# Bucketed attention and a rational feed-forward on one core: the order of each pair's work rewritten, one addition per pair on VectorE, a third buffer for high parts

## The chip, the core and the metric

The kernel runs on one core of a Trainium2 chip. The metric is the device time of one execution in microseconds (us). Three runs of the kernel before gave 961.02, 961.62 and 962.98, a median of 961.62. About 0.2% (2 us) is what a measurement of this kernel can tell from no change.

## What is computed

Attention with a mask from hashed buckets, and a feed-forward with a rational function between its two products (the feed-forward's input is the attention's output, 3072 tokens of 512 features):

```
q, k, v: 4 x 8 heads x 768 tokens x 64;  proj: 64 x 6
q_bucket, k_bucket = the 6 signs of q @ proj, of k @ proj, read as a number
scores = q @ k.T / 8, and -1e9 where the buckets differ
attn = exp(scores - rowmax);  attn = attn / (sum + 1e-9);  x = attn @ v
h = x @ w_in  (512 x 2048)
P = a0 + a1 h + a2 h^2 + a3 h^3;   Q = 1 + |b0||h| + |b1| h^2
out = (P / (Q + 1e-6)) @ w_out  (2048 x 512)
```

## The kernel before

**Pairs.** Two heads make a pair; there are 16 pairs (p = 0 to 15), and a pair's 12 steps s are 2 halves of the queries (hf) by 6 tiles of the keys. Every float32 operand of a large product is split into a high part (a cast to float32r, on ScalarE) and a low part (the rest, a subtraction). A pair's work on TensorE, with the names that the profile shows:

- `pss` (`scores`): the 12 score tiles, transposed, 8 matmuls each: high by high, high by low, low by high, and a product of 13 mask rows (`mask_q`, `mask_k`) that adds the bucket penalty and subtracts the row maximum. ScalarE takes the exponential of both heads' halves into `E` (two ACTIVATE). GpSimd adds the exponentials of three steps in a row into `acc`: for each group of three, one addition `acc<-E,E` and one `acc<-acc,E`, each for two heads.
- `psm` (`maxstep`): for the pair after, 12 products of the high parts and mask rows, 4 matmuls each, whose row maxima VectorE takes (TENSOR_REDUCE into `m`). `combine` joins the two halves of `m`, `pst` (`shift_turn`) transposes `m` on TensorE, VectorE writes it as `mt`, and a DMA (`shift_rows`) carries it into row 12 of `mask_q`, for which the last two of the first score tile's 8 matmuls wait.
- `psv` (`values`): the product with v, one PSUM bank for each half hf. `values_out` copies a bank out on ScalarE (`col`, then `xo`), and SyncE's queue stores `xo`.
- `psu` (`sums`): the column sums of the four `acc`; ScalarE copies them out as `sr`.
- `psb` (`bits`): the signs for the next two pairs, at every second pair.

Beside this run the splits of w_in and w_out (`weights`: `wr`, `ws`, `wi_hi`, `wi_lo`, a chain over ScalarE and VectorE) and, in pairs 13 to 15, the loads of the feed-forward's first tokens (`tokens.load`: `xl`, `xh`, `y`). The feed-forward (`Ffn.step`) follows: 96 steps of 12 matmuls `psh` and 12 matmuls `pso`.

**PSUM.** The pool `ps_b` has four banks with one tag: `pss` takes two for each step, and `psv`, `psu`, `pst` and `psh` one each, so a bank must be copied out before a later product gets it. The pool `ps_a` has two double banks, for `psm` and `psb`.

**What sets the order.** Every engine executes its instructions in program order; `keep_in_program_order` (line 94) keeps them so, and so nearly all rows of the profile show that line. The order is a plan: `at(p, s, f, ...)` puts a call at the time 12 p + s, where s may be any number, and all calls are issued in the order of these times. The numbers stand in three tables: `FIRST` (pair 0 and what comes before it), `MID` (all other pairs) and `LAST` (pair 15, the first feed-forward steps). In `MID`, `values=[11.232, 11.235]` puts both halves of `psv` at a pair's end, `values_out=[13.624, 11.651]` copies half 1 out at once and half 0 after the second score step of the pair after, and `maxima` with `maxima_steps` places the 12 `psm` among the `pss`. A number under 12 by little means the end of the pair, where `psv` runs.

**Buffers.** `operand` gives the high parts, low parts and v two buffers each, by the parity of the pair. `LAST["share"] = 11` gives VectorE the second head's additions from the last step of pair 14 on.

Of the kernel before, what the change touches and what calls it, by code (L numbers as in the profile page):

```python
# [8 lines left out]
F32R = mybir.dt.float32r  # L9
# [4 lines left out]
ALU = mybir.AluOpType  # L14
# [4 lines left out]
P = 128  # L19
S = 768  # L20
HQ = 384
NT = S // P
# [3 lines left out]
NPAIR = B * NHP  # L26
# [12 lines left out]
PINNED = ("tensor", "vector", "scalar", "gpsimd", "sync")  # L39
PARTS = 2  # L40
ACCS = 5

MID = dict(
    values=[11.232, 11.235], values_out=[13.624, 11.651], values_store=[16.343, 19.938], maxima=14.842,
    maxima_steps=[-2.469, 0.405, 5.72, -1.821, 2.012, 3.592, 6.656, 5.98, -0.169, 2.19, 3.044, 4.48], sums=11.885,
    sums_store=23.222, high=[11.3, 11.31], low=[11.4, 11.41], bits=11.165, penalties=11.256, maskrows=11.73, load_v=11.882,
    shift_turn=11.021, shift_rows=11.645, load=13.548, recips=[27.25, 35.733, 50.884],
    weights=[[11.238, 16.003, 11.648, 11.215, 11.243, 12.014, 8.577, 10.628, 84.011], [11.734, 11.024, 8.997, 11.67, 169.938, 19.538, 12.0, 11.386, 11.645]],
    weights_last=[-71.997, -119.997, -119.944, -125.487], combine=11.0,
)  # L50

FIRST = dict(
    maxima1=5.731, rate1=0.618, maxima2=13.527, rate2=0.8, high=[11.6, 11.7], low=[11.8, 11.9], bits=5.355, penalties=11.558,
    maskrows=13.003, load_v=10.702, group=2, values=[4.117, 2.119, 0.719, 4.463, 2.555, 0.675], values_out=1.607,
    high1=[-24.581, -9.069], low1=[-9.075, -7.508], load2=-15.454, load3=-29.223, load4=16.55, penalties1=3.81, maskrows1=5.52,
    weights=[[18.321, 11.519, 4.92, 53.379, 11.911, 106.055, -39.7, 11.558, 22.997], [10.848, 11.998, 30.437, 11.678, 10.699, -4.525, 6.547, 18.997, 11.431]],
    warm=6, warms=[3, 3, 3, 1, 1, 1], maxima00=[-23.897, -20.363, -18.634, -18.631, -17.575, -17.572], shift0=[-15.7, 5.117],
    ahead=3, scores=[-3.723, 19.958, 20.538], pen01=[-14.501, -23.848], comp01=-24.325, load_v0=-15.703, bits1=-14.498,
    comp1=[-9.072, -7.867], maxima0=[-3.224, 4.166, 4.336, -8.151, 3.428, -0.292], turn1=[10.225, 14.098], rows1=[11.995, 15.252],
    combine0=[-17.0, 5.0], combine1=[10.0, 14.0], clear=6.0,  # L60
)

LAST = dict(
    group=6, values=[0.5, 0.106], values_out=0.7, vout14=15.994,
    tokens=[[-0.105, -0.89, -2.003, -10.837], [0.189, 1.726, 6.933, 5.285], [5.282, 0.008, 4.776, -0.407]], terms=-0.578,
    ffn=[10.067, 81.505, 121.388], sums=11.67, wide=12, share=11, third=0, sums14=17.262, sumst14=24.048,
)
TINY = 2.0 ** -80

# [106 lines left out]
def attention(ctx, tc, nc, raw, ps_b, tail, tokens, early, operands_to_terms, ffn, load, QF, KF, v, w_in, w_out, wo_d, ident, cst, ones, prj,  # L176
# [5 lines left out]
    def operand(tag, p, shape, dtype, bufs=2):  # L182
        return opn[(NPAIR - 1 - p) % bufs == 0].tile(shape, dtype, tag=f"{tag}_{p % bufs}", name=f"{tag}_{p}")
# [29 lines left out]
    QH, KH, QL, KL, V, MB, ACC, EXP, AV, MS = ({} for _ in range(10))  # L213
# [10 lines left out]

    def high(p, t):
        F, T, n = ((QF, QH, "qh"), (KF, KH, "kh"))[t]
        T[p] = operand(n, p, [P, S], F32R)
        nc.scalar.copy(T[p], F[p])

    def low(p, t, engine=nc.vector):  # L230
        F, H, T, n = ((QF, QH, QL, "ql"), (KF, KH, KL, "kl"))[t]
        T[p] = operand(n, p, [P, S], F32R)
        engine.tensor_tensor(out=T[p], in0=F[p], in1=H[p].bitcast(F32), op=ALU.subtract)

    def bits(p, which=(0, 1)):
# [26 lines left out]
    def halves(banks, p, units, left, right):  # L262
        for u, (a, b) in enumerate(units):
            for h in range(2):
                r = slice(64 * h, 64 * h + 64)
                nc.tensor.matmul(banks[h][:, 0:HQ], a[p][r, left], b[p][r, right], start=(u == 0), stop=(u == len(units) - 1))
# [84 lines left out]
    def scores(p, s):  # L351
        hf, kt = divmod(s, NT)
        e = EXP[p, s] = E[(12 * p + s) % NE if p < NPAIR - 1 else s % LONE]
        late = 12 * (p - NPAIR + 2) + s
        if late >= LAST["wide"] and late % 3 != LAST["third"]:
            both = ps_a.tile([P, 2, 512], F32, tag="psa", name=f"pss{p}_{s}")
            banks = both[:, 0, :], both[:, 1, :]
        else:
            banks = [ps_b.tile([P, 512], F32, tag="s", bufs=4, name=f"pss{p}_{s}_{h}") for h in range(2)]
        halves(banks, p, ((KH, QH), (KH, QL), (KL, QH), (MK, MQ)), slice(kt * P, kt * P + P), slice(hf * HQ, hf * HQ + HQ))  # L360
        for h in range(2):
            nc.scalar.activation(e[:, h, 0:HQ], banks[h][:, 0:HQ], AF.Exp, scale=1.0 / 8.0)
        n = NT // PARTS
        if kt % n == 1:
            ACC[p, hf, kt // n] = sm.tile([P, 2, HQ], F32, tag="acc", name=f"acc{p}_{hf}_{kt // n}", bufs=ACCS)
        if kt % n > 0:
            acc = ACC[p, hf, kt // n]
            x = EXP[p, s - 1] if kt % n == 1 else acc
            for h in range(2):
                engine = nc.vector if h and late >= LAST["share"] else nc.gpsimd  # L370
                engine.tensor_tensor(out=acc[:, h, :], in0=x[:, h, 0:HQ], in1=e[:, h, 0:HQ], op=ALU.add)

    def values(p, s):
        hf, kt = divmod(s, NT)
        if kt == 0:
            AV[p, hf] = ps_b.tile([P, 512], F32, tag="s", bufs=4, name=f"psv{p}_{hf}")
        e = EXP[p, s]
        for h in range(2):
            nc.tensor.matmul(AV[p, hf][64 * h : 64 * h + 64, 0 : HQ + 1], V[p][:, kt, 64 * h : 64 * h + 64],
                             e[:, h, 0 : HQ + 1], start=(kt == 0), stop=(kt == NT - 1))  # L380
# [89 lines left out]
    def at(p, s, f, *args):  # L470
        plan.setdefault(12 * p + s, []).append((f, args))

    def spread(p, steps, gen):
        for s in steps:
            at(p, s, lambda g: next(g, None), gen)

    for p in range(NPAIR):
        mid = 0 < p < NPAIR - 1
        n = (FIRST if p == 0 else LAST)["group"]
        for s in range(12):  # L480
            if p > 0 or s >= FIRST["ahead"]:
                at(p, s, scores, p, s)

            if p > 1:
                at(p - 2, MID["maxima"] + MID["maxima_steps"][s] if p > 2 else FIRST["maxima2"] + FIRST["rate2"] * s, maxstep, p, s)
            if mid:
                at(p, MID["values"][s // NT], values, p, s)
            elif s % n == n - 1:
                for i in range(s - n + 1, s + 1):
                    at(p, s + (FIRST if p == 0 else LAST)["values"][s // n], values, p, i)  # L490
            if s % NT == NT - 1:
                at(p, LAST["vout14"] if (p, s) == (NPAIR - 2, 11) else MID["values_out"][s // NT] if mid
                   else s + (FIRST if p == 0 else LAST)["values_out"], values_out, p, s // NT)
        for hf in range(2):
            at(p, MID["values_store"][hf] if mid else 6 * hf + 9, values_store, p, hf)
        if p < NPAIR - 1:
            at(p, MID["sums"] if p < NPAIR - 2 else LAST["sums14"], sums, p)
            at(p, MID["sums_store"] if p < NPAIR - 2 else LAST["sumst14"], sums_store, p)
        if p > 1:
            for t in range(2):  # L500
                at(p - 2, (MID if p > 2 else FIRST)["high"][t], high, p, t)
                at(p - 2, (MID if p > 2 else FIRST)["low"][t], low, p, t, nc.vector if p > 2 else nc.gpsimd)
            if p % 2 == 0:
                at(p - 2, (MID if p > 2 else FIRST)["bits"], bits, p)
                at(p - 2, (MID if p > 2 else FIRST)["penalties"], penalties, p)
            at(p - 2, (MID if p > 2 else FIRST)["maskrows"], maskrows, p)
        if p > 0:
            at(p - 1, (MID if p > 1 else FIRST)["load_v"], load_v, p)
        if p > 1:
            at(p - 1, MID["combine"], combine, p)  # L510
            at(p - 1, MID["shift_turn"], shift_turn, p)
            at(p - 1, MID["shift_rows"], shift_rows, p)
        if p > 3:
            at(p - 4, MID["load"] if p > 4 else FIRST["load4"], load, p)
        if p % NHP == NHP - 1 and p + 1 < NPAIR:
            spread(p, MID["recips"], recips(p // NHP))
# [303 lines left out]
```

## Time and profile before

| | before |
|---|---|
| median of 3 runs | 961.62 us |
| the profiled execution, its own time | 961.61 us |
| its span (first to last instruction) | 959.8 us |
| TensorE busy | 935.1 us (97%) |
| VectorE busy | 832.1 us (87%) |
| ScalarE busy | 653.3 us (68%) |
| GpSimd busy | 398.3 us (41%) |
| mean granted TensorE clock | 0.994 |

Some 1.8 us of the execution's time lie outside the span. TensorE is busy nearly all of the time, but its ends are modelled: a matmul that waits for a bank right behind another one shows as a longer matmul, not as idle time. So the start times of matmuls are read below, not the busy share.

### The profile page before, as it was taken

The page shows a single profiled execution, that of the slowest core. Times are in us where ns is not written, and L with a number is a line of the kernel's source. Part 1 is how long each engine was busy: PE and PEld are TensorE (multiplying, and loading weights), DVE is VectorE, ACT ScalarE, POOL GpSimd, SP SyncE. Part 2 cuts the span into 40 slices and gives each one's busy share as a digit, 9 for nine tenths or more (in the row PEclk, how much of TensorE's full clock was granted, in tenths as well). Part 3 has the DMA queues.
Part 4 walks back from the last instruction along what each step waited for, and adds up shares of the span by engine and source line. Part 5 has one row for each costly group of instructions (what it writes and reads, how often), then busy time and mean ns, then how long its engine had stood idle before and what let it go on. Part 6 is the DMA issues. An engine that isn't in the chain of part 4 may idle for free.

```text
span 959.8 us, 15893 instructions
## 1 busy us (share of the span) xinstructions
PE 935.1 (97%) x5846; PEld 721.9 (75%) x5846; DVE 832.1 (87%) x1051; ACT 653.3 (68%) x1225; POOL 398.3 (41%) x373
## 2 busy tenths in 40 slices
PE   8989999999999999799999999999999999999997
PEld 4566776767676767568888788888888888888886
DVE  6787878878787878569999899899989999998995
ACT  4566676767776767378766767777677667767664
POOL 6686565656565656332222232222322222232222
PEclk9999999999999999899999999999999999999999
DMA  6134444444444424145700400120030004001001
GB/s 191 41 113 140 139 140 141 140 141 140 140 140 128 143 90 136 55 142 207 238 27 0 133 1 1 59 74 0 1 109 25 1 1 131 1 1 45 1 1 44
DMA packets 39245, 81.51 MB, mean 85 GB/s; under 512 B 7168, under 2 KB 18036, under 8 KB 39168
## 3 DMA queue, kind: packets, MB, share of 16 engines
q1 hardware_dynamic: 38736, 80.27, 26.3%
q8 instruction: 46, 0.75, 0.3%
q14 instruction: 31, 0.25, 0.1%
q10 hardware_dynamic: 432, 0.23, 0.1%
HBM read 56.82 MB, written 21.17 MB: 81 GB/s over the span
## 4 chain that ended last, share of the span: by engine, by line
PE 92%; ACT 2%; DMA 2%; DVE 1%; issue 1%; SPq 1%; POOL 0%; ACTq 0%; POOLq 0%
PE psh L94 27%; PE pso L94 27%; PE pss L94 14%; PE psv L94 13%; PE psm L94 6%; PE psu L94 2%; ACT E L94 2%; PE psb L94 1%; DVE m L94 1%; DMA out<-o 1%; SPq L94 1%; DMA qkf<-kT 1%; DMA wo_d<-wr 1%; PE pst_None L94 0%; POOL acc L94 0%
## 5 line engine op out<-in xcount | busy, mean ns | idle before, releaser
L94 POOL TENSOR_TENSOR gl<-c,gh 128x512 fp32r<-128x512 f32 x96 | 136.3, 1420 | 385.4 <-ACT gh L94 375.8
L94 PE MATMUL pso<-wo,gh 128*128 128x512 f32 x768 | 235.5, 389 | 1.3 <-ACT o L94 1.3
L94 ACT ACTIVATE E<-pss 128x384 f32<-128x384 f32 x384 | 167.4, 491 | 81.9 <-PE pss L94 75.7
L94 DVE TENSOR_REDUCE m<-psm 128x2 f32<-128x768 f32 x192 | 177.9, 956 | 24.3 <-PE psm L94 17.4
L94 POOL TENSOR_TENSOR acc<-E,E 128x384 f32<-128x384 f32 x124 | 126.7, 1044 | 160.3 <-ACT E L94 158.9
L94 PEld LDWEIGHTS pso<-wo,gh 128*128 128x128 f32 x768 | 144.1, 188 | 31.5 <-ACT o L94 1.7
L94 PE MATMUL psh<-xh,wi_hi 128*128 128x512 f32 x384 | 149.6, 390 | 0.0
L94 PE MATMUL psh<-xl,wi_hi 128*128 128x512 f32 x384 | 149.4, 389 | 0.0
L94 PE MATMUL psh<-xh,wi_lo 128*128 128x512 f32 x384 | 149.4, 389 | 0.0
L94 PE MATMUL pso<-wo,gl 128*128 128x512 f32 x384 | 148.4, 389 | 0.0
L94 ACT ACTIVATE h<-psh 128x512 f32<-128x512 f32 x96 | 57.4, 598 | 128.5 <-PE psh L94 128.5
L94 DVE SCALAR_TENSOR_TENSOR c<-c,ab,r 128x512 f32<-128x512 f32 x96 | 136.7, 1424 | 0.0
L94 PE MATMUL psv<-E,v 128*64 128x385 f32 x768 | 131.4, 495 | 0.0
L94 POOL TENSOR_TENSOR acc<-acc,E 128x384 f32<-128x384 f32 x123 | 122.4, 1018 | 5.7 <-ACT E L94 5.5
L94 PEld LDWEIGHTS psv<-E,v 128*64 128x64 f32 x768 | 71.3, 139 | 52.8 <-issue 34.0
L94 PE MATMUL pss<-qh,kh 64*128 64x384 f32 x384 | 90.8, 358 | 2.4
L94 DVE SCALAR_TENSOR_TENSOR w<-h,absb,w 128x512 f32<-128x512 f32 x96 | 75.0, 782 | 17.9 <-ACT w L94 17.6
L94 PE MATMUL pss<-mask_q,mask_k 64*128 64x384 f32 x384 | 81.0, 337 | 3.2 <-DMA mask_q<-mt_None 3.2
L94 PE MATMUL pss<-ql,kh 64*128 64x384 f32 x384 | 83.9, 345 | 0.0
L94 PEld LDWEIGHTS psh<-xh,wi_hi 128*128 128x128 f32 x384 | 72.1, 188 | 15.7 <-issue 0.9
L94 PEld LDWEIGHTS psh<-xh,wi_lo 128*128 128x128 f32 x384 | 72.1, 188 | 15.2
L94 PEld LDWEIGHTS pso<-wo,gl 128*128 128x128 f32 x384 | 72.0, 188 | 15.1
(89 smaller groups left out, 1674.0 us busy)
## 6 DMA issues: line engine op xcount, KB each, us to landing
wr<-w_in SPq DMA_DIRECT2D x16, 512.0 KB
wr<-w_out SPq DMA_DIRECT2D x16, 512.0 KB
wo_d<-wr SPq DMA_DIRECT2D x16, 512.0 KB
wo<-wo_d SPq DMA_DIRECT2D x16, 512.0 KB
qkf<-qT SPq DMA_DIRECT2D x16, 384.0 KB
qkf<-kT SPq DMA_DIRECT2D x32, 192.0 KB
v<-v SPq DMA_DIRECT2D x16, 384.0 KB
x_d<-xo SPq DMA_DIRECT2D x32, 192.0 KB
```

What stands on the lines that cost most here:

```text
L94: return self.tc.keep_in_program_order(issue(*args, **kwargs))
```

## The change

- The tables `MID`, `FIRST` and `LAST` have new numbers throughout: the same calls at other places. In `MID`, half 1 of `psv` now comes before half 0 (`values`), `pst` stands between them (`shift_turn`), both halves are copied out before the next pair's scores (`values_out`), one `psm` stands behind each `pss` (`maxima_steps`), and the cast of k's high part comes after the tenth score step (`high`). In `LAST`, the first three feed-forward steps stand behind all score and value products of pair 15 (`ffn`).
- The addition of a pair's last exponentials (s = 11, both heads in one instruction of 128 x 768) goes from GpSimd to VectorE for pairs 1 to 14, as a call of its own (`add`).
- The high parts of q and k have three buffers; the low parts of even pairs lie in the pool `raw`, under the tags that the tokens' `y` also uses.

```diff
+VADDS = (11,)
 MID = dict(
-    values=[11.232, 11.235], values_out=[13.624, 11.651], values_store=[16.343, 19.938], maxima=14.842,
-    maxima_steps=[-2.469, 0.405, 5.72, -1.821, 2.012, 3.592, 6.656, 5.98, -0.169, 2.19, 3.044, 4.48], sums=11.885,
+    values=[11.684, 11.138], values_out=[11.884, 11.615], values_store=[14.41, 17.811], maxima=14.89,
+    maxima_steps=[1.089, 3.351, 2.636, 5.192, -0.277, 4.26, 7.788, 8.138, -2.212, 6.928, -0.974, 1.717], sums=11.894,
...
 LAST = dict(
...
-    ffn=[10.067, 81.505, 121.388], sums=11.67, wide=12, share=11, third=0, sums14=17.262, sumst14=24.048,
+    ffn=[167.535, 769.59, 808.64], sums=855.873, wide=12, share=11, third=0, sums14=17.126, sumst14=808.331,
...
     def high(p, t):
         F, T, n = ((QF, QH, "qh"), (KF, KH, "kh"))[t]
-        T[p] = operand(n, p, [P, S], F32R)
+        T[p] = operand(n, p, [P, S], F32R, 3)
...
     def low(p, t, engine=nc.vector):
         F, H, T, n = ((QF, QH, QL, "ql"), (KF, KH, KL, "kl"))[t]
-        T[p] = operand(n, p, [P, S], F32R)
+        own = (NPAIR - 1 - p) % 2 == 0
+        T[p] = operand(n, p, [P, S], F32R) if own else raw.tile([P, S], F32R, tag=f"lo{t}", name=f"{n}_{p}", bufs=1)
...
-        if kt % n > 0:
+        if kt % n > 0 and not (s in VADDS and 0 < p < NPAIR - 1):
...
+    def add(p, s):
+        acc = ACC[p, s // NT, s % NT // (NT // PARTS)]
+        nc.vector.tensor_tensor(out=acc, in0=acc, in1=EXP[p, s][:, :, 0:HQ], op=ALU.add)
...
+            if mid and s in VADDS:
+                at(p, MID["adds"][VADDS.index(s)], add, p, s)
```

What the numbers do to the order stands in the following rows, in which a name ends with a running number. TensorE first, at the end of pair 7 (`psv7_0`, `psv7_1` are its halves, each row two matmuls; `pst8` and `psm8` belong to pair 8). Before:

```order
L94 MATMUL psm8_6_2973<-mask_k2_166,mask_q2_163 128x384 x2
...
L94 MATMUL pss7_11_0_2995<-mask_q1_162,mask_k1_165 128x384
...
L94 MATMUL pst8_None_3010<-cst_76,m0_191 64x128
L94 MATMUL psv7_0_3019<-E0_149,v_7_2739 64x385 x2
...
L94 MATMUL psv7_1_3032<-E6_155,v_7_2739 64x385 x2
...
L94 MATMUL psu7_3073<-acc7_0_0_2784,ones_82 32x384 x2
```

With the change:

```order
L95 MATMUL pss7_11_0_2987<-mask_q1_162,mask_k1_165 128x384
...
L95 MATMUL psm8_7_2999<-mask_k2_166,mask_q2_163 128x384 x2
L95 MATMUL psv7_1_3005<-E6_155,v_7_2692 64x385 x2
...
L95 MATMUL pst8_None_3025<-cst_76,m0_191 64x128
L95 MATMUL psv7_0_3041<-E0_149,v_7_2692 64x385 x2
...
L95 MATMUL psu7_3067<-acc7_0_0_2785,ones_82 32x384 x2
```

The turn `pst8` has moved from before all of `psv` to between its halves, and half 1 runs first.

ScalarE, from the end of pair 7 to the first exponentials of pair 8. Before:

```order
L94 COPY col7_1_3061<-psv7_1_3032 128x1
L94 ACTIVATE xo7_1_3062<-psv7_1_3032,col7_1_3061 128x384
L94 CAST wr15_2958<-ws15_2959 128x512
L94 COPY sr7_3082<-psu7_3073 128x384
L94 ACTIVATE E0_149<-pss8_0_0_3084 128x384
...
L94 ACTIVATE E1_150<-pss8_1_1_3105 128x384
L94 COPY col7_0_3129<-psv7_0_3019 128x1
L94 ACTIVATE xo7_0_3130<-psv7_0_3019,col7_0_3129 128x384
```

With the change:

```order
L95 ACTIVATE xo7_1_3034<-psv7_1_3005,col7_1_3033 128x384
L95 CAST qh_9_3039<-qkf9_2476 128x768
L95 CAST wr15_2764<-ws15_2765 128x512
L95 CAST wi_hi_128<-ws14_2978 128x512
L95 COPY col7_0_3063<-psv7_0_3041 128x1
L95 ACTIVATE xo7_0_3064<-psv7_0_3041,col7_0_3063 128x384
L95 COPY sr7_3076<-psu7_3067 128x384
L95 ACTIVATE E0_149<-pss8_0_0_3083 128x384
```

The copy of half 0 (`xo7_0`) has moved from behind the second score step of pair 8 to before its first.

VectorE between pairs 14 and 15 (`mt15` is the turned maximum of pair 15, `acc14_1_1` the last sum of pair 14, `y0_0` a product of the first tokens). Before:

```order
L94 TENSOR_REDUCE m1_192<-psm15_6_5343 128x2
L94 TENSOR_TENSOR y0_0_5349<-xl0_5161,xh0_5160 128x768
L94 TENSOR_TENSOR acc14_1_1_5363<-acc14_1_1_5363,E11_160 128x384
L94 TENSOR_TENSOR m1_192<-m1_192 128x12
L94 TENSOR_SCALAR mt15_None_5384<-pst15_5382 12x128
```

With the change, and under it the rows of SyncE's queue that lead to the DMA of `mt15`:

```order
L95 TENSOR_REDUCE m1_192<-psm15_7_5366 128x2
L95 TENSOR_TENSOR m1_192<-m1_192 128x12
...
L95 TENSOR_SCALAR mt15_None_5396<-pst15_5394 12x128
...
L95 TENSOR_TENSOR acc14_1_1_5335<-acc14_1_1_5335,E11_160 128x768
...
L95 DMA xl0_3_5426<-x_d3_91 128x512
L95 DMA xh0_3_5425<-r_d0_108 64x512 x2
L95 DMA mask_q0_161<-mt15_None_5396 1x6x128 x2
```

`combine` has moved ahead of the addition of pair 14; on the queue the loads `xl0_3` and `xh0_3` still stand directly ahead of the mask row, as they did before. By the waits in the program, `xl0_3` is issued once the last `psv14` matmul and `acc14_1_1` are done, in both kernels.

## Rows read from the trace of the kernel before

**Rows 1.** The page, part 1: span, and busy time of each engine.

```profile
span 959.8 us, 15893 instructions
...
PE 935.1 (97%) x5846; PEld 721.9 (75%) x5846; DVE 832.1 (87%) x1051; ACT 653.3 (68%) x1225; POOL 398.3 (41%) x373
```

**Rows 2.** Windows by stage: pair 0; 1; 2 to 13; 14 and 15; feed-forward.

```profile
0.00:48.90 48.90, 44.68 (x338) 25.22 (x340) 34.94 (x53) 24.52 (x46) 30.60 (x44) 1.00 0.41 115
48.90:77.80 28.90, 24.93 (x222) 17.48 (x222) 24.66 (x30) 17.56 (x39) 20.26 (x19) 1.00 0.40 125
77.80:375.50 297.70, 295.58 (x2622) 212.82 (x2618) 242.27 (x309) 209.47 (x450) 187.20 (x192) 1.00 0.42 133
375.50:432.60 57.10, 49.73 (x385) 36.39 (x383) 36.56 (x47) 32.37 (x73) 23.96 (x23) 0.91 0.36 111
432.60:957.00 524.40, 520.13 (x2296) 429.97 (x2292) 493.68 (x615) 369.39 (x617) 136.27 (x96) 1.00 0.15 50
```

The columns of Rows 2 are the window and its length, then busy time and instructions of PE, PEld, DVE, ACT and POOL, the granted clock, the DMA share and GB/s.

**Rows 3.** Timeline of TensorE, pair 6's values to pair 8's turn: start, length.

```profile
266.93 7.92 PE L94 MATMUL psv<-E,v 128*64 128x385 f32 x47
...
276.21 0.44 PE L94 MATMUL pss<-qh,kh 64*128 64x384 f32 x2
...
277.37 0.89 PE L94 MATMUL pss<-qh,kh 64*128 64x384 f32 x2
...
285.19 0.34 PE L94 MATMUL pss<-qh,kh 64*128 64x384 f32 x2
...
286.24 0.33 PE L94 MATMUL pss<-qh,kh 64*128 64x384 f32 x2
...
287.45 0.44 PE L94 MATMUL psm<-kh,qh 64*128 64x384 f32 x2
...
290.69 0.43 PE L94 MATMUL pst_None<-cst,m 128*64 128x128 f32 x2
```

**Rows 4.** Timeline of ScalarE in the same stretch.

```profile
277.27 0.88 ACT L94 ACTIVATE E<-pss 128x384 f32<-128x384 f32 x2 [0.39 <-PE pss L94]
...
279.61 0.59 ACT L94 ACTIVATE xo<-psv,col 128x384 f32<-128x384 f32 x1
```

**Rows 5.** Timeline of VectorE: pairs 1, 7, 14 and 15.

```profile
49.64 1.71 DVE L94 CUSTOM_DVE_ANT_0 ws<-wr,ws 128x1024 uint16<-128x1024 uint16 x1 [0.54 <-ACT sr L94]
...
280.56 9.61 DVE L94 TENSOR_REDUCE m<-psm 128x2 f32<-128x768 f32 x10 [0.44 <-PE psm L94]
...
392.37 1.34 DVE L94 TENSOR_TENSOR acc<-acc,E 128x384 f32<-128x384 f32 x1 [1.85 <-POOL acc L94]
...
418.29 0.56 DVE L94 TENSOR_TENSOR acc<-acc,E 128x384 f32<-128x384 f32 x1
```

**Rows 6.** Timeline of TensorE in pair 1.

```profile
54.81 0.40 PE L94 MATMUL pst<-cst,m 128*64 128x128 f32 x2 [1.20 <-DVE m L94]
...
68.25 0.40 PE L94 MATMUL pst_None<-cst,m 128*64 128x128 f32 x2 [2.10 <-DVE m L94]
```

**Rows 7.** Timeline of TensorE between pairs 14 and 15.

```profile
393.94 0.45 PE L94 MATMUL pst<-cst,m 128*64 128x128 f32 x1 [3.99 <-DVE m L94]
...
408.24 1.16 PE L94 MATMUL pss<-mask_q,mask_k 64*128 64x384 f32 x2 [3.17 <-DMA mask_q<-mt_None]
```

**Rows 8.** Windows: the two stretches of low clock (columns as in Rows 2).

```profile
391.00:399.00 8.00, 5.06 (x19) 3.87 (x21) 5.44 (x10) 3.52 (x7) 2.30 (x3) 0.57 0.00 0
408.00:412.30 4.30, 4.03 (x25) 3.77 (x27) 1.98 (x3) 2.54 (x7) 1.01 (x1) 0.60 0.69 204
```

**Rows 9.** Timeline of SyncE's queue: pair 7, and between pairs 14 and 15.

```profile
267.44 1.58 SPq L94 DMA_DIRECT2D mask_q<-mt_None  x2
...
404.46 0.33 SPq L94 DMA_DIRECT2D xl<-x_d  x1
...
406.06 1.55 SPq L94 DMA_DIRECT2D mask_q<-mt_None  x2
```

**Rows 10.** The chain that ended last, between pairs 14 and 15.

```profile
406.06 2.13 DMA mask_q<-mt_None
```

More of the change, by code (lines that the diff above doesn't have):

```diff
@@ L41 @@
 ACCS = 5
+VADDS = (11,)
 MID = dict(
-    values=[11.232, 11.235], values_out=[13.624, 11.651], values_store=[16.343, 19.938], maxima=14.842,
-    maxima_steps=[-2.469, 0.405, 5.72, -1.821, 2.012, 3.592, 6.656, 5.98, -0.169, 2.19, 3.044, 4.48], sums=11.885,
-    sums_store=23.222, high=[11.3, 11.31], low=[11.4, 11.41], bits=11.165, penalties=11.256, maskrows=11.73, load_v=11.882,
-    shift_turn=11.021, shift_rows=11.645, load=13.548, recips=[27.25, 35.733, 50.884],
-    weights=[[11.238, 16.003, 11.648, 11.215, 11.243, 12.014, 8.577, 10.628, 84.011], [11.734, 11.024, 8.997, 11.67, 169.938, 19.538, 12.0, 11.386, 11.645]],
@@ L49 @@
-    weights_last=[-71.997, -119.997, -119.944, -125.487], combine=11.0,
+    values=[11.684, 11.138], values_out=[11.884, 11.615], values_store=[14.41, 17.811], maxima=14.89,
+    maxima_steps=[1.089, 3.351, 2.636, 5.192, -0.277, 4.26, 7.788, 8.138, -2.212, 6.928, -0.974, 1.717], sums=11.894,
+    sums_store=14.997, high=[11.678, 9.702], low=[11.952, 11.874], bits=11.08, penalties=11.084, maskrows=11.881, load_v=11.364,
+    shift_turn=11.469, shift_rows=11.977, load=14.997, recips=[23.927, 35.322, 55.327],
@@ L50 @@
+    weights=[[10.997, 11.997, 11.565, 179.694, 11.509, 11.858, 11.485, 10.284, 865.593], [11.325, 11.725, 11.628, 13.913, 879.87, 11.172, 0.394, 11.155, 11.855]],
+    weights_last=[-134.698, -0.003, -120.0, -869.006], combine=11.172, adds=[11.662],
 )
 FIRST = dict(
-    maxima1=5.731, rate1=0.618, maxima2=13.527, rate2=0.8, high=[11.6, 11.7], low=[11.8, 11.9], bits=5.355, penalties=11.558,
-    maskrows=13.003, load_v=10.702, group=2, values=[4.117, 2.119, 0.719, 4.463, 2.555, 0.675], values_out=1.607,
@@ L55 @@
[L55 to L58, printed above, removed]
@@ L59 @@
-    comp1=[-9.072, -7.867], maxima0=[-3.224, 4.166, 4.336, -8.151, 3.428, -0.292], turn1=[10.225, 14.098], rows1=[11.995, 15.252],
-    combine0=[-17.0, 5.0], combine1=[10.0, 14.0], clear=6.0,
+    maxima1=5.127, rate1=0.677, maxima2=12.804, rate2=0.937, high=[2.549, 0.266], low=[11.68, 11.715], bits=5.525,
+    penalties=9.664, maskrows=10.933, load_v=9.874, group=2, values=[3.491, 1.642, 0.579, 3.401, 2.558, 0.727], values_out=0.891,
+    high1=[-33.057, -32.695], low1=[-31.72, 25.07], load2=-30.033, load3=3.003, load4=33.003, penalties1=3.84, maskrows1=4.581,
@@ new lines @@
+    weights=[[22.225, 9.881, 11.718, 11.891, 11.043, 149.997, 23.169, -56.357, 38.994], [10.211, 12.801, 117.815, -56.338, -54.382, 11.567, -52.133, 11.73, 3.0]],
+    warm=6, warms=[3, 3, 3, 1, 1, 1], maxima00=[-33.07, -33.057, -39.179, -33.066, -39.176, -33.059], shift0=[22.444, 5.568],
+    ahead=3, scores=[25.073, 27.088, 28.003], pen01=[-34.282, -39.151], comp01=-43.535, load_v0=24.263, bits1=-29.13,
+    comp1=[20.074, 22.587], maxima0=[1.293, -0.795, 3.656, 4.864, 3.787, 4.203], turn1=[10.441, 14.104], rows1=[11.9, 16.555],
@@ L61 @@
+    combine0=[-32.349, 4.981], combine1=[10.214, 12.997], clear=-0.607,
 )
 LAST = dict(
-    group=6, values=[0.5, 0.106], values_out=0.7, vout14=15.994,
-    tokens=[[-0.105, -0.89, -2.003, -10.837], [0.189, 1.726, 6.933, 5.285], [5.282, 0.008, 4.776, -0.407]], terms=-0.578,
-    ffn=[10.067, 81.505, 121.388], sums=11.67, wide=12, share=11, third=0, sums14=17.262, sumst14=24.048,
+    group=6, values=[0.134, 0.54], values_out=0.731, vout14=15.036,
+    tokens=[[-0.313, -0.709, -3.003, 0.003], [5.131, 5.728, -1.165, 3.114], [9.008, 3.305, 10.003, -0.13]], terms=-0.174,
```

## The prediction

> **What bounds the kernel now.** The page's first part comes first: TensorE is busy for 935.1 of 959.8 us, VectorE for 832.1, ScalarE for 653.3 and GpSimd for 398.3 [rows 1]. By these shares there would be 25 us to win at most. But a busy share is a mean over stages, and a matmul that waits for a PSUM bank counts as busy, so the next view is the windows by stage [rows 2]. Pairs 2 to 13 take 297.7 us, 24.8 each, with TensorE at 295.58. Pair 0 leaves it idle for 48.90 - 44.68 = 4.2 us, pair 1 for 28.90 - 24.93 = 4.0, pairs 14 and 15 for 57.10 - 49.73 = 7.4 at a granted clock of 0.91, the feed-forward for 4.3 of 524.4. So the feed-forward is at TensorE's own rate, and what an order can give lies in the attention.
>
> Third comes the timeline of TensorE in one pair, for the starts of the matmuls [rows 3]. A score step with its maximum step takes 1.05 us when nothing holds it (285.19 to 286.24). Twelve of them would take 12 x 1.05 = 12.6, yet from the first `pss` at 276.21 to the next pair's `pst` at 290.69 there are 14.48. The stall of 1.9 us hides inside matmuls that read as longer: `pss` at 277.37 shows 0.89 where a free one shows 0.34. ScalarE tells why [rows 4]: half 0 of the values is copied out (`xo`) only at 279.61, behind the exponentials of two steps. Until then one of the four banks is taken, so the scores have three where two steps want four, and each step waits for the exponentials of the one before. A second, smaller part is two `psm` in a row (287.45, 0.44 instead of 0.34), which wait for a bank that VectorE's reduction, 0.96 each [rows 5], has to free.
>
> Fourth, the waits at the edges: in pair 1, `pst` waits 1.20 and 2.10 us for VectorE's `m` [rows 6]; between pairs 14 and 15, 3.99 for `m`, then 3.17 for the DMA of the mask row [rows 7]. After both the clock is low, 0.57 and 0.60 over 8.0 and 4.3 us [rows 8].
>
> **The change, part by part.** The profiled execution took 961.61 us, the median 961.62, so the sum needs no correction; 1.8 us lie outside the span.
>
> *Pairs 2 to 13.* Both copies of the values now stand before the pair's first exponentials, and `sr` too, so the scores start with four banks; one `psm` follows each `pss`, so no doubled step is left. What ends the stall is 14.48 - 12.6 = 1.9 a pair [rows 3]. What can take its place is ScalarE's queue in front of the first exponential. Half 0 now ends with psv: 7.92 us after its start [rows 3]. Then `col`, `xo` (0.59, [rows 4]) and `sr` stand before E, some 1.6 us, and psu covers 1.36 of it (276.21 - 266.93 - 7.92) and the first step 1.05. That fits. VectorE pays more: its last low part (kl, ql) and the new addition stand ahead of the first reduction. By the order it ends them about when the first `psm` is there, so I leave 0.3 of the stall and take 1.6. Twelve pairs: 12 x 1.6 = **19.2**. Ends: 12 x 0.5 = 6, if only the doubled `psm` (2 x 0.27) goes, and 12 x 1.75 = 21.
>
> *The addition.* One instruction of 128 x 768 replaces two of GpSimd. No row shows it; an addition of 128 x 384 took 0.56 alone and 1.34 while GpSimd was at work [rows 5]. Twice that gives 1.1 and 2.7. I take 1.1: GpSimd has two additions less a pair and has ended those of step 10 while psv runs. It costs TensorE nothing as long as it ends before the last group of psu reads it, nine us after the start of psv. Without that cover it would put up to 2.7 us on VectorE's 242.27 / 12 = 20.2 a pair [rows 2] (first rival). Below nothing it cannot go.
>
> *The turn.* `pst` now stands between the halves of psv. So the mask row has half of psv (7.92 / 2), psu (1.36) and the six matmuls that come first in a score tile (0.5, half of a step's twelve in 1.05) as cover: 5.8 us, where all of psv gave it 9.8. SyncE issues one mask row in 0.79 [rows 9], and issue to landing took 2.13 [rows 10]. In the new queue the four rows of `maskrows` stand directly ahead of the turn's two, at every second pair behind v's load too. They wait for the signs, not for the turn, and can go out while half 1 runs. Were all four still to go when `mt` is there, 4 x 0.79 + 2.13 = 5.3 would just fit; with them gone some 2 to 3 us are left. Cost nothing; the cover is the second half of psv, and without it the price is rival B's.
>
> *The third buffer.* It lets k's cast come at the tenth step instead of in psv. It is the same 0.87-sized work on ScalarE, which has 297.7 - 209.47 = 88 us free over the twelve pairs [rows 2]. Nothing by itself; what it takes from psv's stretch is part of the 1.6.
>
> *Pair 1.* VectorE's two long pieces of weights (`ws`, 1.71, [rows 5]) no longer stand ahead of the joined maxima. The waits of 1.20 and 2.10 [rows 6] go, 3.3, and part of the same stall inside the scores, 1.2: **4.5**. Ends 2 (a smaller wait is left) and 5.5.
>
> *Pair 0.* All places are new. Its idle 4.2 us [rows 2] can't all go, since the first loads are in it. Ends: -4 and +2 (a wait of pair 1's size at a new place); I take a gain of **2**, as the product of the signs now fills one of the waits.
>
> *Pairs 14 and 15.* `combine` moves ahead of the addition of pair 14 and of `y0_0`. At 392.37 that addition stood 1.85 us for GpSimd and took 1.34 [rows 5], `y0_0` before it; with both behind, the wait of 3.99 [rows 7] goes. Of the low clock after it: 8.0 us at 0.57 are 1.1 at full and 6.9 at half; TensorE was busy for 5.06 [rows 8], so at least 4.0 at half speed, which lost 2.0. With 1.6 from the scores of pair 14 this is 4.0 + 2.0 + 1.6 = **7.6**. Ends 1.6 and 8. The second wait stays: `xl` at 404.46 still stands ahead of the mask row, and by the program it waits for the last product and addition of pair 14, so the row goes out at 406.06 as before [rows 9], and 3.17 and the clock of 0.60 are paid again.
>
> *Feed-forward.* The first three `psh` move behind the values of pair 15. The same matmuls on an engine that is busy for 520.13 of 524.4 [rows 2]: nothing. Ends -1.5 and +2, should the first w_out load come late.
>
> The sum: 19.2 + 4.5 + 2 + 7.6 = 33.3, and 961.6 - 33.3 = **928.3 us**.
>
> **Rivals.** *A: VectorE takes over.* The addition meets GpSimd and takes 2.7: 22.9 a pair where it is busy for 20.2 of 24.8 now [rows 2]. Where 1.1 of the 4.6 us that it stands idle are left, its period is 24.0, and a pair gains 0.8 instead of 1.6: 12 x 0.8 = 9.6 less, 937.9. For it: 832.1 us busy [rows 1] and the 1.34 of 392.37. Against it: GpSimd has 110 us free in this stretch (297.7 - 187.20). The Trainium skill (SBUF — State Buffer, section "Who interferes with whom") speaks for it: a VectorE instruction with two inputs in SBUF contends with a GpSimd instruction that reads SBUF, and whoever comes first blocks the other fully. The rows agree, 1.34 against 0.56; by that rule the addition is dear exactly if GpSimd's of step 10 still runs, and then 937.9 is the time.
>
> *B, slower: the mask row lands late.* All pairs but the first turn their maxima with 5.8 us of cover instead of 9.8. If the row lands more than 5.8 us after `pst`, TensorE stops in the first score tile, at every pair. The spot was seen once: 3.17 of wait [rows 7], then 4.3 us at 0.60 [rows 8], of which 3.4 were at half speed and lost 1.7. At that size in 13 pairs, 13 x 4.9 = 64: 992. It decides from a delay of 2 to 3 us on: the signs' rows or v's load ahead of it on SyncE (as the load at 404.46 held the row), or VectorE late to `mt`, ahead of which it now has two pieces of w_out's split. Against it: what stands ahead of the turn's rows in pairs 2 to 13 waits for nothing of the same moment, unlike that load.
>
> *C: the edges give nothing.* A new wait of about the old size takes the place of that before `pst15`, and pairs 0 and 1 move theirs: 19.2 + 1.6, so 940.8. For it: the waits are VectorE's, and it has more to do.
>
> *D: the change doesn't do what it says.* The banks are free earlier, but ScalarE, with 0.88 for each step's exponentials and three copies before them [rows 4], comes as late to the first E as before. Then the edges alone give 14.1: 947.5. Against it: 209.47 busy of 297.7.
>
> **How the numbers follow.** The forecast has 0.60, A 0.15, C 0.10, D 0.04, B 0.06; 0.05 is left for gains and waits that cancel, 0.03 of it within 0.2% (some 2 us, about what a measurement of this kernel can tell from no change) and 0.02 slower. Faster is then 0.60 + 0.15 + 0.10 + 0.04 = 0.89, same 0.03, slower 0.08. The range goes down to 918: the upper ends of the terms, 21 + 5.5 + 4 + 8, give 923, and 5 more could come from the 24.8 - 14.48 - 7.92 - 1.36 = 1.0 us a pair that lie outside scores, values and sums. It goes up to 944, which takes in A, C and the middle pairs at their lower end (6 + 14.1, so 941.5); about 2 in 10 lie outside.
>
> **What would show it.** In the new profile, psv should start every 23.2 us on average (24.8 - 1.6), and `pss` of the second step show no 0.89; E should start right behind `sr`. The new `acc<-acc,E` of 128x768 should show 1.1; 2.7, with VectorE's reductions waiting for nothing while TensorE waits for `m`, is A. A wait of `pss<-mask_q,mask_k` for the DMA in the middle pairs is B. Between pairs 14 and 15 one low stretch should be left, that of the mask row, near 3 us of wait; two are C. A feed-forward window off 524.4 by over 2 us would make that part wrong, and E starting a microsecond after its product would be D.

## The result

The changed kernel takes 928.20 us (median of 4 runs, 926.03 to 928.38), the kernel before 961.32 on the same chip: a ratio of 0.9647, with a 95% interval of 0.9629 to 0.9665. The forecast was 928.3. The profiled execution is the fastest of the four, 926.03 us with a span of 924.0. Of the ten executions of one kernel below (the early copy with the addition on VectorE), the two that lay over 1.5% above its fastest are left out of its numbers.

The page's first part, after:

```profile
span 924.0 us, 15831 instructions
PE 911.4 (99%) x5846; PEld 725.1 (78%) x5846; DVE 836.8 (91%) x1064; ACT 654.4 (71%) x1225; POOL 364.9 (39%) x346
```

Where the time went shows in windows cut at the same events in both kernels: the first score matmul of pair 2, of pair 14 and of pair 15, and the start of pair 14's `psu`, which runs among the scores of pair 15. After (columns as in [rows 2]):

```profile
0.00:69.68 69.68, 67.86 (x557) 44.21 (x558) 55.71 (x84) 43.11 (x87) 46.20 (x60) 1.00 0.41 123
69.68:348.59 278.91, 278.88 (x2620) 218.81 (x2616) 248.28 (x321) 210.41 (x450) 158.41 (x168) 1.00 0.46 144
348.59:369.79 21.20, 21.20 (x198) 17.41 (x194) 20.20 (x26) 14.83 (x33) 13.24 (x14) 1.00 0.52 175
369.79:378.02 8.23, 4.97 (x50) 4.26 (x49) 3.81 (x6) 4.58 (x13) 2.02 (x2) 1.00 0.45 154
```

And before, cut at the same events:

```profile
0.00:77.79 77.79, 69.60 (x557) 42.69 (x558) 59.59 (x82) 42.08 (x85) 50.86 (x62) 1.00 0.40 119
77.79:375.44 297.65, 295.53 (x2621) 212.77 (x2617) 242.21 (x309) 209.47 (x450) 187.20 (x192) 1.00 0.42 133
375.44:404.27 28.83, 24.66 (x198) 20.25 (x194) 20.27 (x27) 15.57 (x34) 14.86 (x15) 0.88 0.28 84
404.27:414.13 9.86, 6.66 (x49) 5.83 (x48) 2.38 (x3) 4.34 (x12) 2.03 (x2) 0.83 0.66 195
```

The first stage gives 77.79 - 69.68 = 8.1 us, pairs 2 to 13 give 297.65 - 278.91 = 18.7, pair 14 gives 7.6 and the first scores of pair 15 give 1.6. From there to the end it is 0.3 the other way (959.8 - 414.13 = 545.7, and 924.0 - 378.02 = 546.0). The sum is 35.8, the difference of the spans.

In a middle pair TensorE's timeline shows what answers to [rows 3]. After, at the start of pair 8's scores and at their end:

```profile
209.14 0.44 PE L95 MATMUL pss<-qh,kh 64*128 64x384 f32 x2
...
210.29 0.34 PE L95 MATMUL pss<-qh,kh 64*128 64x384 f32 x2
...
222.04 1.57 PE L95 MATMUL psb<-qkf,prj 128*32 128x384 f32 x16
```

The second step shows 0.34 where 0.89 stood, and the stage takes 222.04 - 209.14 = 12.9 us, near the unstalled 12.6 and far from 14.48. ScalarE's timeline gives the reason [rows 4]: `xo` of half 0 and `sr` come out before the first `E`, which waits for TensorE alone:

```profile
208.09 0.58 ACT L95 ACTIVATE xo<-psv,col 128x384 f32<-128x384 f32 x1
209.33 0.48 ACT L95 COPY sr<-psu 128x384 f32<-128x384 f32 x1 [0.66 <-PE psu L95]
210.20 1.87 ACT L95 ACTIVATE E<-pss 128x384 f32<-128x384 f32 x4 [0.38 <-PE pss L95]
```

Between pairs 14 and 15 the wait for `m` is gone and the one for the mask row stays, 3.25 us [rows 7], since the load still stands ahead of it on SyncE's queue [rows 9]. First TensorE, then the queue:

```profile
373.84 0.77 PE L95 MATMUL pss<-mask_q,mask_k 64*128 64x384 f32 x2 [3.25 <-DMA mask_q<-mt_None]
```

```profile
370.01 0.33 SPq L95 DMA_DIRECT2D xl<-x_d  x1
370.38 1.09 SPq L95 DMA_DIRECT2D xh<-r_d  x2
371.52 1.55 SPq L95 DMA_DIRECT2D mask_q<-mt_None  x2
```

### The profile page after: what moved, and what is told of

It is laid out like the page before. It is cut to its first block, busy times and chain, and to the rows that moved or that the text cites. A ratio compares the mean times of both kernels' runs of the same rounds, so it can differ in the third digit from the quotient of the medians.

```text
span 924.0 us, 15831 instructions
## 1 busy us (share of the span) xinstructions
PE 911.4 (99%) x5846; PEld 725.1 (78%) x5846; DVE 836.8 (91%) x1064; ACT 654.4 (71%) x1225; POOL 364.9 (39%) x346
## 4 chain that ended last, share of the span: by engine, by line
PE 94%; DMA 1%; ACT 1%; DVE 1%; SPq 1%; issue 0%; ACTq 0%; DVEq 0%
PE psh L95 28%; PE pso L95 28%; PE pss L95 13%; PE psv L95 13%; PE psm L95 7%; PE psu L95 2%; PE psb L95 1%; SPq L95 1%; DMA out<-o 1%; PE psw L95 1%; DVE m L95 0%; DMA v<-v 0%; ACT E L95 0%; DVE ws L95 0%; PE pst L95 0%
## 5 line engine op out<-in xcount | busy, mean ns | idle before, releaser
L95 DVE TENSOR_REDUCE m<-psm 128x2 f32<-128x768 f32 x192 | 182.7, 959 | 19.4 <-PE psm L95 5.3
L95 POOL TENSOR_TENSOR acc<-E,E 128x384 f32<-128x384 f32 x124 | 124.4, 1030 | 158.7 <-ACT E L95 157.8
L95 DVE SCALAR_TENSOR_TENSOR c<-c,ab,r 128x512 f32<-128x512 f32 x96 | 138.7, 1445 | 0.0
L95 POOL TENSOR_TENSOR acc<-acc,E 128x384 f32<-128x384 f32 x96 | 90.6, 970 | 2.2 <-ACT E L95 2.0
L95 DVE SCALAR_TENSOR_TENSOR w<-h,absb,w 128x512 f32<-128x512 f32 x96 | 72.9, 759 | 15.9 <-ACT w L95 15.6
L95 PEld LDWEIGHTS psh<-xl,wi_hi 128*128 128x128 f32 x384 | 72.1, 188 | 14.9
L95 DVE SCALAR_TENSOR_TENSOR w<-w,r 128x512 f32<-128x512 f32 x96 | 78.5, 818 | 0.0
L95 ACT ACTIVATE c<-psh,ab 128x512 f32<-128x512 f32 x96 | 75.4, 785 | 0.8 <-POOL gl L95 0.7
```

The source lines that it names most:

```text
L95: return self.tc.keep_in_program_order(issue(*args, **kwargs))
```

## The experiments

Every kernel was timed beside the kernel before on its own chip, whose median lay between 961.3 and 963.4 us; so ratios are compared, and starts and windows of one profile each. A difference in us to the changed kernel is one of medians, which by the ratios comes out up to 1.6 us otherwise.

### One part of the gain taken back at a time

**Half 0 copied out late.** The changed kernel with

```diff
-    values_out=[11.884, 11.615]
+    values_out=[13.624, 11.615]
```

> The changed kernel with half 0 of the values copied out behind the second score step of the pair after, as before. Theory (banks: the late copy leaves three PSUM banks to the scores): the waits of the second and third score step come back, 0.4 + 0.3 and some 0.2 behind them, about 0.9 in each of 13 pairs, +12 us (9 to 15), near 940; pss of the second step shows 0.8 to 0.9 again. Rival (the places of the maximum steps make the gain): within 3 us of 928.2.

Measured: 937.68 us, ratio 0.9744 (0.9729 to 0.9760), 9.5 us over the changed kernel. The stall came back where it had been; its timeline, pair 8:

```profile
215.28 0.44 PE L95 MATMUL pss<-qh,kh 64*128 64x384 f32 x2
...
216.43 0.89 PE L95 MATMUL pss<-qh,kh 64*128 64x384 f32 x2
...
217.87 0.82 PE L95 MATMUL pss<-qh,kh 64*128 64x384 f32 x2
```

In the kernel before the same two steps show 0.89 [rows 3] and 0.84:

```profile
278.80 0.84 PE L94 MATMUL pss<-qh,kh 64*128 64x384 f32 x2
```

Pairs 2 to 13 take 290.0 us (69.59 to 359.61) instead of 278.9. So the late copy is a cause, at 0.9 us a pair.

**The old places of the maximum steps.** The changed kernel with `maxima` and `maxima_steps` of before.

```diff
-    maxima=14.89, maxima_steps=[1.089, 3.351, 2.636, ...
+    maxima=14.842, maxima_steps=[-2.469, 0.405, 5.72, ...
```

> The changed kernel with the old numbers for the maximum steps (two in a row twice a pair, the last one elsewhere). Theory (banks): two doubled steps of 0.27 a pair and a later joined maximum, +4 to +9 us, 932 to 937. Rival (the places of the maximum steps make the gain): +15 us or more, above 943.

Measured: 938.04 us, ratio 0.9744 (0.9727 to 0.9761), 9.8 us more. That is just above the end of my range, 937, and below the rival's bound: these places carry about as much as the copy does (pairs 2 to 13 take 287.9, from 70.52 to 358.45). The doubled steps are only a part of it, two of 0.17 in pair 9; there the last score step also stands right behind the one before, its first product shows 0.57 where a free one shows 0.34, and psv starts some 0.5 later.

**The addition back on GpSimd.**

```diff
-VADDS = (11,)
+VADDS = ()
```

> The changed kernel with the addition of step 11 on GpSimd again, two of 128x384. Theory (the addition is off the path on either engine): 927 to 930, and psu follows psv with no wait. Rival (GpSimd's last additions end too late or meet VectorE's in psv's stretch): psu waits for acc by 0.5 us or more in every pair, 934 or more.

Measured: 934.80 us, ratio 0.9709 (0.9690 to 0.9728): 6.6 us over the changed kernel and beyond my range, at the rival's number, though not by the rival's way: `psu` does not wait. What waits is `pst`, for `m`, in every second pair (0.65 to 0.76 us; these pairs take 23.4 instead of 22.4; of the others, pairs 6 and 10 lose 0.8 and 0.7, the rest nothing). VectorE's timeline names the cause. With the addition back, VectorE and then GpSimd, end of pair 5:

```profile
155.12 3.70 DVE L95 TENSOR_TENSOR m<-m 128x12 f32<-128x12 f32 x1
158.74 0.42 DVE L95 TENSOR_SCALAR wr<-wr 128x512 int32<-128x512 int32 x1
```

```profile
155.04 1.97 POOL L95 TENSOR_TENSOR acc<-E,E 128x384 f32<-128x384 f32 x2
156.98 1.81 POOL L95 TENSOR_TENSOR acc<-acc,E 128x384 f32<-128x384 f32 x2
```

`combine`, an instruction over 12 columns, takes 3.70 us and ends 0.03 after GpSimd's fourth addition in a row (156.98 + 1.81 = 158.79). Its readers, `pst` first, wait that long:

```profile
158.88 0.32 PE L95 MATMUL pst_None<-cst,m 128*64 128x128 f32 x1 [0.76 <-DVE m L95]
```

In the changed kernel the same instruction took at most 1.92 in the 14 pairs, over two additions, and no `pst` waited:

```profile
107.71 1.92 DVE L95 TENSOR_TENSOR m<-m 128x12 f32<-128x12 f32 x1
```

```profile
107.61 2.00 POOL L95 TENSOR_TENSOR acc<-E,E 128x384 f32<-128x384 f32 x2
```

Pairs 2 to 13 lose 11.1, 9.0 and, here, 7.2 us (69.63 to 355.76) in the three kernels, 27 in all, more than the 18.7 that they gained: the parts are not additive. Any one stall that is left takes a good part of the whole.

### The early copy alone

The kernel before with one number changed:

```diff
-    values_out=[13.624, 11.651]
+    values_out=[11.655, 11.651]
```

> The kernel before with one number changed: half 0 of the values is copied out together with half 1, ahead of the pair's first exponentials. Theory (banks): 0.9 a pair is won, -9 to -15 us against before, near 950, and the second pss shows 0.34 to 0.5 instead of 0.89. Rival: no gain, since ScalarE's copy then delays the first exponential or the doubled maximum steps hold the pair anyway: within 3 us of 961.3.

Measured: 968.45 us, ratio 1.0063 (1.0047 to 1.0079): slower than before. Theory and rival had both missed it. Most pairs gained 0.4 us (25.2 and 23.6 by turns, where the kernel before takes 25.6 and 24.0), but pairs 8 and 9 took 30.4 and 29.0. VectorE, GpSimd and TensorE at the end of pair 8:

```profile
239.12 4.25 DVE L94 TENSOR_TENSOR m<-m 128x12 f32<-128x12 f32 x1
```

```profile
239.56 2.00 POOL L94 TENSOR_TENSOR acc<-E,E 128x384 f32<-128x384 f32 x2
241.48 1.86 POOL L94 TENSOR_TENSOR acc<-acc,E 128x384 f32<-128x384 f32 x2
```

```profile
243.52 0.66 PE L94 MATMUL pst_None<-cst,m 128*64 128x128 f32 x2 [3.86 <-DVE m L94]
```

`combine` again ends with GpSimd's last addition (241.48 + 1.86 = 243.34, and 239.12 + 4.25 = 243.37). In the other pairs from 2 to 13 of the same run it took 0.5 while GpSimd went on for 3.6 us and more: it had got its turn between two additions. VectorE and GpSimd at the end of pair 4:

```profile
141.61 0.54 DVE L94 TENSOR_TENSOR m<-m 128x12 f32<-128x12 f32 x1
```

```profile
140.28 1.85 POOL L94 TENSOR_TENSOR acc<-acc,E 128x384 f32<-128x384 f32 x2
142.07 1.98 POOL L94 TENSOR_TENSOR acc<-E,E 128x384 f32<-128x384 f32 x2
```

The Trainium skill (SBUF — State Buffer, section "Who interferes with whom") says that a VectorE instruction with two inputs in SBUF contends with a GpSimd instruction that reads SBUF, and that the one which comes first blocks the other fully. The rows agree, and they add that the wait can last over four additions in a row.

**A combine that needs one input.** To test this hold by itself, `combine` was written as a reduction over the two halves, into columns of its own; it takes the same maxima (its readers and the width of `m` follow, not shown):

```diff
-        nc.vector.tensor_tensor(out=m[:, c : c + n], in0=m[:, c : c + n], in1=m[:, 2 * NT + c : 2 * NT + c + n], op=ALU.max)
+        nc.vector.tensor_reduce(out=m[:, 4 * NT + c : 4 * NT + c + n],
+            in_=m[:, 0 : 4 * NT].rearrange("p (t c) -> p c t", t=2)[:, c : c + n, :], axis=AX.X, op=ALU.max)
```

> The early copy in the kernel before, with combine as a reduction with one input (over the two halves, into columns of m of their own) in place of an addition's two inputs. Theory (a VectorE instruction with two inputs in SBUF stands until GpSimd's queue of additions is empty; this made combine 4.25 us long in two pairs): combine takes under 0.5 in every pair, the two pairs with 5.4 us more go, so some 11 us less than the early copy alone, 3 to 6 us under before (ratio 0.994 to 0.997). Rival (VectorE or the maxima are late there for another reason): the two long pairs stay, ratio 1.004 or more.

Measured: 954.52 us, ratio 0.9930 (0.9913 to 0.9947). The two long pairs are gone and `combine` is short:

```profile
162.09 0.18 DVE L94 TENSOR_REDUCE m<-m 128x12 f32<-128x24 f32 x1
```

So it is the hold that made the early copy slower: every pair now takes 25.0 or 23.4 by turns, 0.6 us less than before. Of these, 0.4 stood already in the free pairs of the early copy; the other 0.2 came with the shorter `combine` (0.18 instead of 0.5), and what it would give without the early copy no run shows.

**The addition on VectorE.** The early copy and the new `add` at 11.6585, nothing else.

```diff
+VADDS = (11,)
...
+            if mid and s in VADDS:
+                at(p, 11.6585, add, p, s)
```

> The early copy in the kernel before, with the addition of step 11 on VectorE as in the changed kernel and nothing else. Theory (the same lock): with two additions less on GpSimd combine stays under 2 us, no pair stands for 3.9, ratio to before 0.990 to 0.996. Rival: the long pairs stay, ratio 1.004 or more.

Measured: 965.05 us, median of 8 runs that lie between 957.0 and 969.3; ratio 1.0023 (0.9996 to 1.0050). In the profiled execution no pair stands for 3.9, but three of them for 2.1, each with a `combine` of about 2.5 that ends with GpSimd:

```profile
139.96 2.48 DVE L95 TENSOR_TENSOR m<-m 128x12 f32<-128x12 f32 x1
```

```profile
140.43 1.99 POOL L95 TENSOR_TENSOR acc<-E,E 128x384 f32<-128x384 f32 x2
```

The gain of my theory is not there; the interval reaches into the rival's range, 1.004 or more, but its long pairs have become shorter ones. Moving one addition is no cure by itself: in the other pairs from 2 to 13 of this execution `combine` took 0.5, so it got its turn in most and not in all. That this chance also makes the spread of the 8 runs is likely and not shown, since only one has rows.

**One input, with the addition back on GpSimd,** in the changed kernel (both edits above).

> The changed kernel with the addition of step 11 on GpSimd again, and combine as a reduction with one input. Theory (the added addition costs by the wait of combine for GpSimd, 3.7 us in every second pair): combine under 0.5, no wait for m at pst, ratio to before 0.964 to 0.967 as the changed kernel. Rival (GpSimd is late for its own readers, or holds VectorE's other two-input work): ratio 0.969 or more, as with combine left alone.

Measured: 935.10 us, ratio 0.9722 (0.9707 to 0.9736), no better than with `combine` left alone. My theory falls here. One half of it came true: `combine` takes 0.18, `pst` waits in none of the pairs 2 to 13, and every second of them takes 22.4 again, as in the changed kernel. But four of the others lose 0.8 to 1.7 us (283.9 in all, where 286.1 with `combine` left alone), and the time is at the rival's number: GpSimd stops VectorE's next instruction instead, one with one input, not with two as the rival had it. End of pair 5, VectorE, GpSimd and ScalarE:

```profile
155.15 0.18 DVE L95 TENSOR_REDUCE m<-m 128x12 f32<-128x24 f32 x1
156.06 3.08 DVE L95 TENSOR_SCALAR wr<-wr 128x512 int32<-128x512 int32 x1 [0.73 <-ACT ws L95]
```

```profile
157.01 1.81 POOL L95 TENSOR_TENSOR acc<-acc,E 128x384 f32<-128x384 f32 x2
```

```profile
163.67 0.62 ACT L95 CAST wr<-ws 128x512 fp32r<-128x512 f32 x1 [3.96 <-DVE ws L95]
164.20 0.61 ACT L95 CAST wi_hi<-ws 128x512 fp32r<-128x512 f32 x1
164.72 0.15 ACT L95 COPY col<-psv 128x1 f32<-128x1 f32 x1
164.90 0.58 ACT L95 ACTIVATE xo<-psv,col 128x384 f32<-128x384 f32 x1
```

`wr`, 0.42 us where nothing holds it, takes 3.08 and ends 0.32 behind GpSimd's last addition. Behind it come `ws`, ScalarE's two casts, and only then half 0's copy, at 164.90, whose bank the next scores want: TensorE waited 0.62 for it at 165.54. The pairs agree: those that lose time, 4, 6, 10 and 12, are the ones ahead of whose scores `wr` took 3.05 to 3.08; ahead of pairs 8 and 14 it took 1.20, and pair 8 loses nothing. So what the added addition buys is that GpSimd's queue ends two additions sooner, and VectorE's work beside psv is held for less time.

### The other parts

**Two buffers for the high parts,** k's cast at the pair's end behind q's, pair 2's casts at the end of pair 0:

```diff
-        T[p] = operand(n, p, [P, S], F32R, 3)
+        T[p] = operand(n, p, [P, S], F32R, 2)
-    high=[11.678, 9.702]
+    high=[11.678, 11.69]
-    high=[2.549, 0.266]
+    high=[11.6, 11.65]
```

> The changed kernel with two buffers for the high parts: k's cast at the pair's end behind q's, pair 2's casts at the end of pair 0. Theory (the third buffer moves work that is hidden anyway): 927.5 to 930.5. Rival (the cast in psv's stretch makes ScalarE late for half 0's copy and the first exponentials, so the buffer carries part of the gain): 0.5 us or more a pair, above 934.

Measured: 927.56 us, ratio 0.9625 (0.9610 to 0.9641), which overlaps the changed kernel's. The third buffer is worth nothing that can be measured here.

**The turn behind both halves of the values.**

```diff
-    shift_turn=11.469
+    shift_turn=11.7
```

> The changed kernel with pst behind both halves of psv, so that the mask row has psu and six matmuls as cover, 1.9 us instead of 5.8. Theory (cover decides): the row lands some 3 to 3.5 us after pst, so each of 13 pairs waits 1.1 to 1.6 at pss<-mask_q,mask_k: +14 to +21 us, 942 to 949; if the clock falls after each such wait as it did after the wait of 3.2, some 1.7 more for each, up to 970. Rival (the row's way is short enough): within 3 us of 928.2.

Measured: 941.43 us, ratio 0.9768 (0.9752 to 0.9784), some 12 us over the changed kernel by the ratios (0.0121 x 962) and 13 by the medians, a little under the 14 that I gave. The wait stands where rival B of the prediction had put it; TensorE, pair 6:

```profile
169.13 0.44 PE L95 MATMUL pss<-mask_q,mask_k 64*128 64x384 f32 x1
169.92 0.44 PE L95 MATMUL pss<-mask_q,mask_k 64*128 64x384 f32 x1 [0.35 <-DMA mask_q<-mt_None]
```

The row shows 0.35 idle, and the matmul starts 0.79 after the one of the other head. Pairs 2 to 13 are 1.2 us longer on average (293.8 from 69.47 to 363.27). Ten of them lose 0.9 to 1.1, at the lower end of the 1.1 to 1.6; pairs 2 and 8 lose 2.6 and 1.8, with longer waits for DMAs. The granted clock of the stretch stayed at 1.00 over these short waits:

```profile
69.47:363.27 293.80, 287.35 (x2620) 205.35 (x2616) 248.22 (x322) 211.88 (x450) 158.55 (x168) 1.00 0.44 137
```

**The table of pair 0.** The changed kernel with `FIRST` of before, 9 lines of numbers.

> The changed kernel with the table FIRST of the kernel before (pair 0 and what comes before it). Theory (most of the gain up to pair 2 lies in pair 0's order and in the weights' pieces that FIRST places): +4 to +8 us, ratio to before 0.969 to 0.973. Rival (the gain there is MID's): within 3 us of the changed kernel, ratio 0.964 to 0.968.

Measured: 939.00 us, ratio 0.9760 (0.9746 to 0.9775), some 11 us over the changed kernel, more than expected. Pair 2's scores start at 81.31 instead of 69.68, and later than in the kernel before, 77.79. The old places bring their waits back, and a new one of 3.21 for pair 2's mask rows, behind which the clock was 0.62:

```profile
56.23 1.42 PE L95 MATMUL psm<-mask_k,mask_q 64*128 64x384 f32 x2 [3.21 <-DMA mask_k<-mb]
```

```profile
54.00:62.00 8.00, 5.66 (x28) 4.55 (x30) 2.27 (x4) 1.10 (x4) 2.76 (x3) 0.62 0.21 69
```

So the gain up to pair 2 needs that table, but part of these 11 us, the 3.5 beyond 77.79, comes from two tables that don't fit each other.

**combine first, in the kernel before:**

```diff
-    combine=11.0
+    combine=10.995
-    tokens=[[-0.105, -0.89, -2.003, -10.837]
+    tokens=[[-0.105, -0.89, -0.95, -10.837]
```

> The kernel before with two numbers changed: combine goes ahead of the last addition of pair 14 and of y0_0. Theory: the wait of 3.99 at pst15 falls to under 1, and the low clock after it goes: -4 to -6 us, 955.3 to 957.3; the second wait of 3.2 stays. Rival (VectorE itself is late there): less than 1 us gained.

Measured: 955.22 us, ratio 0.9916 (0.9901 to 0.9931), 8.2 us under the kernel before on its chip and so beyond the 4 to 6 that I gave. In its profile pair 14 takes 22.6 us, from the first score matmul at 374.08 to that of pair 15 at 396.64, instead of 28.83: the 6.3 of the wait and the slow clock behind it, won with two numbers. I had overlooked that the number of `combine` holds for all pairs: in pair 1 it now stands ahead of a part of the weights' split (`wi_lo`), the wait of `pst` falls from 2.10 [rows 6] to 0.83, and pair 2 starts 1.3 earlier. The second wait stays:

```profile
400.73 0.80 PE L94 MATMUL pss<-mask_q,mask_k 64*128 64x384 f32 x2 [3.29 <-DMA mask_q<-mt_None]
```

**The mask row ahead of the load, in the changed kernel:**

```diff
-    tokens=[... [9.008, 3.305, 10.003, -0.13]]
+    tokens=[... [9.008, 3.305, 10.003, -0.015]]
```

> The changed kernel with one number moved: the loads xl0_3 and xh0_3 of the first tokens stand behind the mask row of pair 15 on SyncE's queue. Theory (the load, which waits for the last product of pair 14, holds the row): the wait of 3.25 at pss<-mask_q,mask_k of pair 15 goes, and with it the low clock behind it in the executions that show one (about 2): -3 to -5.5 us, 922.7 to 925.2. Rival (something else is late just then, mt or the first feed-forward loads): the wait shrinks by less than 1 us or comes back later, 927 to 928.4.

Measured: **921.99 us** (921.79 to 922.28), ratio 0.9572 (0.9557 to 0.9586), which beats both kernels. The queue sends the row out at once, and TensorE goes through without a stop:

```profile
366.51 1.61 SPq L95 DMA_DIRECT2D mask_q<-mt_None  x2
370.00 0.33 SPq L95 DMA_DIRECT2D xl<-x_d  x1
```

```profile
370.48 0.34 PE L95 MATMUL pss<-mask_q,mask_k 64*128 64x384 f32 x2
```

6.2 us between the medians (7.2 by the ratios) is more than the upper end of 5.5 that I gave. The spans of the two profiles, 924.0 and 919.9, differ by 4.1; that of the changed kernel is its fastest, 2.2 under the others.

## Why the prediction was right, and where its steps were not

- **The time, 928.3 against 928.2, and its stages.** Pairs 2 to 13: 19.2 forecast, 18.7 measured. Pair 14: 7.6 and 7.6. Pairs 0 and 1 together: 6.5 and 8.1, within the ends. The second wait was to stay and stayed, 3.25. The feed-forward, with the rest of pair 15, was to give nothing and took 0.3. The stages and their mechanism were right; that the medians agree to 0.1 us is luck, since the terms miss by up to 1.6, the stages of the rows give 35.8 where the sum has 33.3, and the median lies 2.2 over the execution that has these rows.
- **The middle pairs.** The late copy was named as the main cause of the stall and is one: undone, it costs 9.5 us in all. But I gave the doubled maximum steps only the smaller part, 2 x 0.27 a pair, and undone they cost 9.8. The 1.6 a pair was right because it came from the whole stall (14.48 against 12.6), not from the split into causes.
- **The addition: the step that was wrong.** Its price was 1.1 and it took 0.95, so that end held:

```profile
206.67 0.95 DVE L95 TENSOR_TENSOR acc<-acc,E 128x768 f32<-128x768 f32 x1
```

  But "it costs TensorE nothing" was all that I said of it, and what it takes off GpSimd was given no worth. It is worth 6.6 us: without it GpSimd's last additions hold VectorE's `combine`, or what comes next, for 3 to 4 us. In the kernel before `combine` took 0.3, so this is no stall that was removed, but one that the new order would have brought and that the prediction did not list: 7.2 us over the twelve pairs, 0.6 of the 1.6 a pair, hang on the addition. I had weighed what the Trainium skill says of the two engines for the added instruction alone, and it decides at another one.
- **The third buffer and the turn.** Nothing for the buffer: right. The mask row's cover of half of psv was enough in pairs 2 to 14. With 3.9 us less of it, most pairs lost 0.9 to 1.1, so some 2.9 had been left, as the prediction's 2 to 3 said; rival B's price of 4.9 a pair was too high for a small delay.
- **The clock.** I let the low clock after the second wait stay. In the profiled execution it did not fall (1.00 from 369.79 to 378.02, against 0.83 before); the other three executions took 2.2 us longer at a lower mean clock (0.997 to 0.998 against 0.999). That is near the 1.7 that the low stretch cost by the prediction's working, but that it came back there is not shown: only the profiled one has rows.

## What to carry to other kernels

Read TensorE's stalls from the starts of its matmuls, and size them as a whole: causes that overlap can't be split by their waits, and one of them alone may bring nothing or make it slower. Where an instruction of 12 columns takes microseconds on VectorE, look at what GpSimd runs and whether both end together: then shorten GpSimd's queue ahead of it, and follow what moves up behind. On a queue that keeps its order, put what the next stage waits for ahead of what waits itself: one number gave some 6 us here.

## What the runs showed of the hardware that was not expected

`combine`, 128x12 with two inputs, took between 0.16 and 4.25 us; the same work with one input took 0.18. A `wr` of 128x512 with one input and integer data, in the same place, took 3.08 instead of 0.42. Either GpSimd stood idle or `combine` got in behind the addition that was running, and it took under 1.0; or it waited until GpSimd had none left: in the nine runs that show any of over 1.0 us there are 44, and each ended within 0.04 us of the last addition in a row, the next one being over 8 us off. What decides between the two is open. The early copy with the addition on VectorE, in which both happened, ran between 957.0 and 969.3 us on one chip.
